# Loading one group's keys and queries as two halves, a value load moved ahead of a weight load, and six dummy matmuls fewer

## The chip, the cores and the metric

The kernel runs on one core of one Trainium2 chip. The metric is the device time of one execution, in microseconds (us). Before the change it is 399.24 us, the median of three runs (399.11 to 399.49). All runs quoted here count as fast (none is over 1.5% above the fastest of its kernel).

## The reference

Attention with eight heads over 4 batches of 768 rows feeds a mixture of four experts. Heads 0, 2 and 6 ("retrieval") are causal over everything. The other five ("stream") see four sink rows and a window of 64.

```python
# q, k, v: (4, 8, 768, 64)
scores = (q @ k.transpose(0, 1, 3, 2)) / 8
mask   = causal                            # heads 0, 2, 6
mask   = causal & (is_sink | in_window)    # the other heads
a      = softmax(where(mask, scores, -1e9))
x      = (a @ v).transpose(0, 2, 1, 3).reshape(3072, 512)
p      = domain_probs / domain_probs.sum(-1)
out    = sum(p[:, e] * (relu(x @ w1[e]) @ w2[e]) for e in range(4))
# w1[e]: (512, 1024), w2[e]: (1024, 512)
```

## The kernel before

The rows are worked on in eight groups of 384. For each group and each expert TensorE does 32 matmuls of the first layer (line L895) and 24 of the second (L919). The attention of group g+1 is interleaved into the experts of group g, so TensorE always has something to do, if the data is there. GpSimd issues the loads, in program order:

```python
    load_v(0, 0, [2, 1, 3, 4, 6])
    load_w1(0, 0, F)
    load_v(0, 0, [5, 7])
    load_w2(0)
    ...
    load_w1(1, 0, F)
    landed(w1_of(0))
    load_triples(k, k16, 0, 1)      # keys of group 1, all heads
    load_triples(q, qt16, 0, 1)     # queries of group 1, all heads
    landed(w2_of(0))
    load_w2(1)
    landed(qt16[0:1, 0, 0, 0:1])
    load_v(0, 1, RH)                # retrieval heads 0, 2, 6
    load_w1(2, 0, F)
    landed(w2_of(1))
    load_v(0, 1, SH[:2])            # stream heads 1, 3
    load_w2(2)
    load_v(0, 1, SH[2:])            # stream heads 4, 5, 7
    landed(w1_of(2))
    load_w1(3, 0, F)
    load_w2(3)
    # ... then, in the group loop, the keys, queries and values of group 2
```

`landed(x)` is a GpSimd copy of one element of a load's target, so GpSimd waits there for that load. One expert's `load_w1` is two loads (half the partitions each), `load_w2` is one. Below, w1(2) means the first-layer weights of expert 2.

For groups 0 and 1 TensorE transposes the keys and queries itself; from group 2 on the DMA does it, on SyncE's queue:

```python
        for j in range(3):
            nc.sync.dma_start(out=qTs[b, c][...], in_=q16[b, c][...], transpose=True)
        for x, xr in ((kR[i][:, c], kRr), (windows(kSf, c), kSr)):
            nc.sync.dma_start(out=x..., in_=xr..., transpose=True)
```

In the first attention TensorE runs dummy matmuls ahead of some heads' values, so that it isn't idle while it waits:

```python
            if first:
                warm_up(ps, {3: 4, 4: 4, 5: 6, 7: 10}.get(h, 0), 256)
```

The last tile of all is done in two column halves of 256, so that the first half's store starts sooner. A number `begin` for each group says after how much expert work the next group's attention is mixed in.

The softmax here doesn't subtract the row's maximum and nothing guards it: scores larger than these inputs give would overflow.

Of the kernel before, what the change touches and what calls it, by code (L numbers as in the profile page):

```python
# [17 lines left out]
def kernel(  # L18
# [33 lines left out]
    nc = tc.nc  # L52
    P = 128
    B, H, S, D = q.shape
    E, DM, F = moe_w1.shape
    CH = 3 * P
    NCH = S // CH
    N = B * S
    HP = H // 2
# [9 lines left out]
    RH = [h for h in range(H) if RETR[h]]  # L69
# [80 lines left out]
    def half(u):  # L150
        return slice(u * D, (u + 1) * D)
# [5 lines left out]
    def own_v(h):  # L157
        return half(PLACE[h][1])
# [10 lines left out]
    def v_tiles(b, c, h):  # L169

        if RETR[h]:
            return vR[b % 2][:, 3 * c : 3 * c + 3, RH.index(h), :]
        if b:
            return windows(vSf, c)[:, :, SH.index(h), :]
        return vS[:, c, :, SH.index(h), :]
# [10 lines left out]
    def rows_of(x, b, h, c):  # L186
        return x[b, h, c * CH : (c + 1) * CH, :].rearrange("(j p) d -> p j d", p=P)

    def tiles_of(x, b, h, c):
        return x[b, h, c * CH : (c + 1) * CH, :].rearrange("(t r) d -> r t d", r=TK)  # L190

    def windows_of(x, b, h, c):

        assert b > 0
        first = ((b * H + h) * S + c * CH - WO) * D
        return bass.AP(x.tensor, x.offset + first, [[D, P], [WQ * D, WT], [1, D]])
# [10 lines left out]
        q16[b, c] = att.tile([P, 3, H, D], FP16, name="q16", bufs=2)  # L207
        load_by_rows(q, q16[b, c], b, c)

    def load_triples(x, dst, b, c):  # L210

        gp.dma_start(
            out=dst.rearrange("p h j d -> p h (j d)"),
            in_=x[b, :, c * CH : (c + 1) * CH, :].rearrange(
                "h (p j) d -> p h (j d)", j=3
            ),
        )
# [47 lines left out]
    def load_v(b, c, heads):  # L265
        for h in heads:
            t = v_tiles(b, c, h)
            if RETR[h]:
                gp.dma_start(out=t[:, :, 0:D], in_=rows_of(v, b, h, c))  # L269
            elif b:  # L270
                gp.dma_start(  # L271
                    out=t[:, :, own_v(h)], in_=windows_of(v, b, h, c)
                )
            else:
                gp.dma_start(  # L275
                    out=t[R0:P, :, own_v(h)],
                    in_=tiles_of(v, b, h, c),
                )
# [18 lines left out]
    def load_w1(e, f0, f1):  # L297
        x = moe_w1[e].rearrange("(u c d) f -> u d c f", u=2, c=DMP)
        for u in range(2):
            gp.dma_start(  # L300
                out=w1sb[half(u), e * DMP : (e + 1) * DMP, f0:f1],
                in_=x[u, :, :, f0:f1],
            )
# [47 lines left out]
    for h in range(H):  # L351
        if h == 2:
            nc.sync.dma_start(
                out=v_s32, in_=v[0, :, 0:NS, :].rearrange("h r d -> r h d")
# [13 lines left out]
        eng = nc.scalar if h < HP else nc.sync  # L368
        eng.dma_start(out=q32[:, :, h, :], in_=rows_of(q, 0, h, 0))
    nc.sync.dma_start(  # L370
        out=probs, in_=moe_domain_probs.rearrange("(t p) e -> p t e", p=P)
# [14 lines left out]
    def warm_up(ps, n, cols):  # L386
        for _ in range(n):
            nc.tensor.matmul(
                out=ps[:, 0:cols], lhsT=warm[:, 0:P], rhs=warm[:, 0:cols],
                start=True, stop=True,  # L390
            )
# [53 lines left out]

    mask_c(bC, 0.0, -60000.0)
    mask_s(bS[:, 0:2, :], 2, 0.0, -60000.0)
    load_v(0, 0, [2, 1, 3, 4, 6])
    load_w1(0, 0, F)
    load_v(0, 0, [5, 7])  # L450
    load_w2(0)
    zero(gp, kR[0][:, 1, :, :, :])
    zero(gp, kS[:, 1, :, :, :].rearrange("p t s x -> p s t x"))
# [1 line left out]
    k16 = att.tile([P, H, 3, D], FP16, name="k16", bufs=1)  # L455
    qt16 = att.tile([P, H, 3, D], FP16, name="q16", bufs=2)

    def landed(x):

        gp.tensor_copy(out=seen, in_=x)  # L460
# [4 lines left out]
    def w2_of(e):  # L465
        return w2sb[0:1, e * FTP, 0:1]

    load_w1(1, 0, F)
    landed(w1_of(0))
    load_triples(k, k16, 0, 1)  # L470
    load_triples(q, qt16, 0, 1)
    landed(w2_of(0))
    load_w2(1)
    landed(qt16[0:1, 0, 0, 0:1])
    load_v(0, 1, RH)
    load_w1(2, 0, F)
    landed(w2_of(1))
    load_v(0, 1, SH[:2])
    load_w2(2)
# [15 lines left out]
    def attention(b, c):  # L495
        g = b * NCH + c
# [212 lines left out]
        def values(h):  # L709
            if RETR[h]:  # L710
                yield from values_r(h)
                return
            ct, u = PLACE[h]
            if first and u == 1:
                ps = pO.tile([P, 512], FP32, name="pO", bufs=2)
            else:
                ps = pV.tile([P, 512], FP32, name="pV", bufs=2)
            if first:
                warm_up(ps, {3: 4, 4: 4, 5: 6, 7: 10}.get(h, 0), 256)
            work = []  # L720
            for es, parts in es_of[h]:
                for t, o, q0, nq in parts:
                    work.append((es, t, o, q0, nq))
            ns = 0
            for n, (es, t, o, q0, nq) in enumerate(work):
                nc.tensor.matmul(  # L726
                    out=ps[:, q0 : q0 + nq],
                    lhsT=v_tile(b, c, h, t),
                    rhs=es[:, o : o + nq],
                    start=(n == 0),  # L730
                    stop=(n == len(work) - 1),
                    skip_group_check=True,
                )
                ns += mm_ns(nq)
                if ns > 300 and n < len(work) - 1:
                    yield ns
                    ns = 0

            r, o = half(u), half(1 - u)
            pair = first and h in (3, 4)  # L740
            if not pair or u == 0:
                rc_of[0] = att.tile([P, CH], FP32, name="rc", bufs=4)
            rc = rc_of[0]
            nc.scalar.activation(  # L744
                out=rc[r, :], in_=ps[o, 0:CH], func=AF.Ln, bias=eps[o, :]
            )

            def scale(r=r, ps=ps):
                nc.vector.tensor_tensor(  # L749
                    out=xT[g][r, ct, :], in0=ps[r, 0:CH], in1=rc[r, :], op=ALU.mult  # L750
                )

            if not pair:
                nc.scalar.activation(out=rc[r, :], in_=rc[r, :], func=AF.Exp, scale=-1.0)  # L754
                later(scale)
            elif u == 0:
                scale_of[0] = scale
            else:
                nc.scalar.activation(out=rc, in_=rc, func=AF.Exp, scale=-1.0)
                later(scale_of[0])  # L760
                later(scale)

            yield ns + (600.0 if g == 1 else 0.0)
# [92 lines left out]

    def last_tile(e, nt, hs, acc):

        for n, eng in enumerate((nc.sync, nc.scalar)):
            cols = slice(n * DM // 2, (n + 1) * DM // 2)  # L860
            ps = pV.tile([P, 512], FP32, name="pV", bufs=2)
            for ft in range(FTP):
                nc.tensor.matmul(
                    out=ps[:, 0 : DM // 2],
                    lhsT=hs[:, ft, 2 * P : 3 * P],
                    rhs=w2sb[:, e * FTP + ft, cols],
                    start=(ft == 0),
                    stop=(ft == FTP - 1),
                )
            nc.vector.scalar_tensor_tensor(  # L870
                out=acc[:, cols], in0=ps[:, 0 : DM // 2],
                scalar=p_sb[:, nt, e : e + 1], in1=acc[:, cols],
                op0=ALU.mult, op1=ALU.add,
            )
            eng.dma_start(out=out[nt * P : (nt + 1) * P, cols], in_=acc[:, cols])


    acc = {}
# [88 lines left out]
    UNIT = FTP * DMP * mm_ns(CH) + 3 * FTP * mm_ns(DM)  # L967
    for g in range(G):
        nxt = g + 1
        n_units = len(units[g])  # L970
        att_steps = iter(())
        if nxt < G:
            att_steps = attention(nxt // NCH, nxt % NCH)
        loads(g + 2)

        begin = {0: 1.15, 1: 1.0}.get(g, 0.0) * UNIT
        end = {0: 3.5}.get(g, 0.90 * n_units) * UNIT

        att_ns = 3500.0 if nxt % NCH == 0 else 5600.0
        if nxt < NCH:  # L980
            att_ns += 1100.0 + HP * 3 * 400.0 + NSH * 600.0
        spent = 0.0
        done = 0.0
        to_transpose = g + 2 < G
        for ns, share in moe_steps(units[g]):

            spent += ns * (share if g == 0 else 1.0)
            tick(ns)
            if to_transpose and spent > {0: 0.9, 1: 0.75}.get(g, 0.5) * n_units * UNIT:
                dma_transposes(*divmod(g + 2, NCH))  # L990
                to_transpose = False
            while done < (spent - begin) / (end - begin) * att_ns:
                step = next(att_steps, None)
                if step is None:
                    break
                done += step
                tick(step)
        for ns in att_steps:
            tick(ns)
        tick(LAG)  # L1000
# [35 lines left out]
```

## Time and profile before

| | before | where it is read |
|---|---|---|
| time, profiled run | 398.83 us | run |
| span | 397.1 us | cores |
| TensorE busy | 388.2 us | busy times |
| first L895 of group 0 | 22.09 us | TensorE timeline |
| w2(1), w1(2), w2(2), w2(3) landed | 39.8, 46.7, 53.2, 64.8 us | issue plus time to landing |
| start of the x32 block (32 matmuls in one row of the view) of L895 of group 1's first expert | 74.30 us | TensorE timeline |
| wait for group 2's transposed keys | 0.17 us, until 85.67 | TensorE timeline |

The main views are in the prediction. This is the timeline of GpSimd before (start, length, what was issued, and in brackets the idle time before it and what ended it):

```profile
41.71 0.91 POOL L306 DMA_DIRECT2D w2sb<-in_moe_w_dram  x1
...
65.13 1.02 POOL L227 DMA_DIRECT2D kSr<-in_k_dram  x1 [3.58 <-DMA w2sb<-in_moe_w_dram]
```

The load of w2(2) is issued at 41.71 with no wait. The last key load of group 2 is held 3.58 us by w2(3). No data pass between those two: the awaited load is the eighth before this one. The packed traces show why: GpSimd's loads, 144 before and 146 after, report their landing on eight semaphores (numbers 110 to 117), strictly in turn, and a load that has to wait is issued some 0.3 us after the load eight places ahead of it has landed (in the first 80 us of all fourteen profiles). Everything that GpSimd issues after this load moves with w2(3).

### The profile page before, as it was taken

How to read it: one execution, taken by the hardware profiler on the slowest of the kernel's cores; microseconds unless marked ns; L12 is line 12 of the kernel's file. 1: busy time of each engine (PE TensorE's matmuls, PEld its weight loads, DVE VectorE, ACT ScalarE, POOL GpSimd, SP SyncE). 2: the span in 40 equal slices, each digit the busy share in tenths (PEclk: the TensorE clock that was granted, in tenths of full speed). 3: DMA queues.
4: the chain of work that ended last, by engine and by line, in shares of the span. 5: the costliest groups of instructions: out<-in, count | busy, mean ns of one | idle time of the engine just before them, and what ended most of it. 6: DMA issues, size and time to landing. Idle time of an engine off the chain costs nothing.

```text
span 397.1 us, 7140 instructions
## 1 busy us (share of the span) xinstructions
PE 388.2 (98%) x2829; PEld 220.7 (56%) x2829; DVE 156.0 (39%) x344; ACT 219.0 (55%) x468; POOL 143.7 (36%) x184
## 2 busy tenths in 40 slices
PE   7899999999999999999999999999999999999996
PEld 4654556545555555555555555555555555555553
DVE  7734765324442234434332333433443223422222
ACT  4754569444766546655765446745564456853331
POOL 8833796808908706900049202940000000000000
PEclk9999999999999999999999999999999999999999
DMA  9999999999999999970779959990472000020002
GB/s 172 158 208 192 178 197 172 139 199 128 128 191 149 121 149 106 141 90 12 141 80 175 65 99 118 112 153 12 83 117 83 2 12 1 11 79 2 0 2 80
DMA packets 166133, 42.23 MB, mean 106 GB/s; under 512 B 156396, under 2 KB 161108, under 8 KB 166100
## 3 DMA queue, kind: packets, MB, share of 16 engines
q0 software_dynamic: 102656, 20.98, 62.0%
q1 hardware_dynamic: 61700, 20.27, 26.5%
q10 hardware_dynamic: 1744, 0.52, 0.6%
q8 instruction: 22, 0.36, 0.4%
q14 instruction: 11, 0.09, 0.1%
HBM read 43.57 MB, written 6.29 MB: 126 GB/s over the span
## 4 chain that ended last, share of the span: by engine, by line
PE 78%; DMA 15%; POOL 6%; issue 1%; DVE 0%; POOLq 0%
PE pA L895 35%; PE pO L919 35%; DMA w1sb<-in_moe_w_dram 4%; DMA w2sb<-in_moe_w_dram 4%; PE pA L614 4%; DMA q<-in_q_dram 3%; DMA kR<-kRr 2%; POOL vR L269 2%; PE pV L726 1%; PE pV L662 1%; DMA vS<-in_v_dram 1%; POOL w1sb L300 1%; POOL vS L275 1%; POOL vS L326 0%; POOL q L201 0%
## 5 line engine op out<-in xcount | busy, mean ns | idle before, releaser
L895 PE MATMUL pA<-xT,w1sb 128*128 128x384 f16 x1024 | 185.9, 326 | 0.1
L919 PE MATMUL pO<-w2sb,hs 128*128 128x512 f16 x760 | 179.0, 379 | 0.8 <-DMA w2sb<-in_moe_w_dram 0.8
L908 ACT ACTIVATE hs<-pA 128x384 f16<-128x384 f32 x256 | 121.8, 492 | 94.9 <-PE pA L895 89.6
L895 PEld LDWEIGHTS <-w1sb 128*128 128x128 f16 x1024 | 95.8, 98 | 59.6 <-issue 0.5
L919 PEld LDWEIGHTS <-hs 128*128 128x128 f16 x760 | 70.7, 98 | 73.9 <-DMA w2sb<-in_moe_w_dram 1.2
L632 ACT ACTIVATE es<-pA 128x384 f16<-128x384 f32 (+2 forms) x122 | 60.1, 512 | 53.7 <-PE pA L614 52.4
L935 DVE SCALAR_TENSOR_TENSOR acc<-pO,p_sb,acc 128x512 f32<-128x512 f32 x71 | 53.3, 751 | 71.8 <-PE pO L919 71.3
L227 POOL DMA_DIRECT2D kSr<-in_k_dram x30 | 30.1, 1006 | 31.5 <-DMA kS<-kSr 22.1
L223 POOL DMA_DIRECT2D kRr<-in_k_dram x18 | 14.1, 785 | 67.7 <-DMA kR<-kRr 67.7
L749 DVE TENSOR_TENSOR xT<-pV,rc 64x384 f16<-64x384 f32 x37 | 20.5, 554 | 32.0 <-ACT rc L754 24.3
L271 POOL DMA_DIRECT2D vS<-in_v_dram x30 | 30.4, 1024 | 0.8 <-DMA q<-in_q_dram 0.8
L931 DVE TENSOR_SCALAR acc<-pO,p_sb 128x512 f32<-128x512 f32 x24 | 18.0, 751 | 28.8 <-PE pO L919 28.6
L636 DVE TENSOR_TENSOR es<-es,mC 128x256 f16<-128x256 f16 (+1 forms) x42 | 10.9, 258 | 45.4 <-ACT es L632 44.3
L744 ACT ACTIVATE rc<-pV,eps 64x384 f32<-64x384 f32 x37 | 21.3, 575 | 12.1 <-PE pV L726 11.5
L614 PE MATMUL pA<-qT,kR 128*128 128x384 f16 (+2 forms) x120 | 24.4, 278 | 0.9 <-ACT qT L525 0.4
L754 ACT ACTIVATE rc<-rc 64x384 f32<-64x384 f32 x38 | 19.8, 521 | 1.2
L269 POOL DMA_DIRECT2D vR<-in_v_dram x24 | 19.2, 802 | 0.4 <-issue 0.3
L726 PEld LDWEIGHTS <-vS 128*128 128x128 f16 x255 | 13.4, 98 | 7.7 <-DMA vS<-in_v_dram 2.1
L636 DVE TENSOR_TENSOR es<-es,mW 128x384 f16<-128x384 f16 x30 | 10.7, 358 | 16.9 <-ACT es L632 16.8
L614 PEld LDWEIGHTS <-kR 128*128 128x128 f16 x120 | 11.4, 98 | 10.6 <-DMA kR<-kRr 0.6
L662 PEld LDWEIGHTS <-es 128*128 128x128 f16 x252 | 13.2, 97 | 6.9 <-ACT es L632 0.6
L614 PEld LDWEIGHTS <-kS 128*128 128x128 f16 x255 | 13.3, 98 | 6.6
(102 smaller groups left out, 188.4 us busy)
## 6 DMA issues: line engine op xcount, KB each, us to landing
out_dram<-acc SPq DMA_DIRECT2D x23, 256.0 KB
w1sb<-in_moe_w_dram POOLq DMA_DIRECT2D x8, 512.0 KB, 9.4
w2sb<-in_moe_w_dram POOLq DMA_DIRECT2D x4, 1024.0 KB, 13.2
kSr<-in_k_dram POOLq DMA_DIRECT2D x30, 112.0 KB, 3.8
vS<-in_v_dram POOLq DMA_DIRECT2D x30, 112.0 KB, 5.6
q<-in_q_dram POOLq DMA_DIRECT2D x18, 128.0 KB, 4.3
vR<-in_v_dram POOLq DMA_DIRECT2D x24, 48.0 KB, 4.4
kRr<-in_k_dram POOLq DMA_DIRECT2D x18, 48.0 KB, 3.7
```

Of the source, the lines that this page charges most:

```text
L227: gp.dma_start(out=kSr[:, :, SH.index(h), own(h)], in_=windows_of(k, b, h, c),)
L269: gp.dma_start(out=t[:, :, 0:D], in_=rows_of(v, b, h, c))
L271: gp.dma_start(out=t[:, :, own_v(h)], in_=windows_of(v, b, h, c))
L614: nc.tensor.matmul(out=ps[:, o : o + nq], lhsT=key_tile(b, c, h, t), rhs=qTs[b, c][:, hp, q0 : q0 + nq], start=(n == 0 or not first), stop ...
L632: nc.scalar.activation(out=es[:, 0:cols], in_=ps[:, 0:cols], func=AF.Exp, scale=SC)
L636: nc.vector.tensor_tensor(out=es[:, o0:o1], in0=es[:, o0:o1], in1=m[:, mo : mo + o1 - o0], op=ALU.mult,)
L744: nc.scalar.activation(out=rc[r, :], in_=ps[o, 0:CH], func=AF.Ln, bias=eps[o, :])
L749: nc.vector.tensor_tensor(out=xT[g][r, ct, :], in0=ps[r, 0:CH], in1=rc[r, :], op=ALU.mult)
L895: nc.tensor.matmul(out=pss[ft][:, 0:CH], lhsT=w1sb[:, e * DMP + ct, ft * P : (ft + 1) * P], rhs=xT[g][:, ct, :], start=(n == 0), stop=(n = ...
L908: nc.scalar.activation(out=hs[:, ft, :], in_=ps[:, 0:CH], func=AF.Relu)
L919: nc.tensor.matmul(out=ps_o, lhsT=hs[:, ft, j * P : (j + 1) * P], rhs=w2sb[:, e * FTP + ft, :], start=(ft == 0), stop=(ft == FTP - 1),)
L935: nc.vector.scalar_tensor_tensor(out=acc[nt], in0=ps_o, scalar=p_ap, in1=acc[nt], op0=ALU.mult, op1=ALU.add,)
```

## The change

The intent: let the first expert start sooner, let w2(1) land sooner, and pay for it with queries that are needed later.

```diff
-    def load_triples(x, dst, b, c):
+    def load_triples(x, dst, b, c, h0, h1):       # heads h0 to h1 only
 ...
-    load_v(0, 0, [2, 1, 3, 4, 6])
+    load_v(0, 0, [2, 1, 3, 4, 6, 5])
     load_w1(0, 0, F)
-    load_v(0, 0, [5, 7])
+    load_v(0, 0, [7])
 ...
-    load_triples(k, k16, 0, 1)
-    load_triples(q, qt16, 0, 1)
+    load_triples(k, k16, 0, 1, 0, HP)             # heads 0 to 3
+    load_triples(q, qt16, 0, 1, 0, HP)
     landed(w2_of(0))
     load_w2(1)
     landed(qt16[0:1, 0, 0, 0:1])
-    load_v(0, 1, RH)
     load_w1(2, 0, F)
+    load_v(0, 1, RH[:2])
+    load_triples(k, k16, 0, 1, HP, H)             # heads 4 to 7
+    load_triples(q, qt16, 0, 1, HP, H)
+    load_v(0, 1, RH[2:])
 ...
-                warm_up(ps, {3: 4, 4: 4, 5: 6, 7: 10}.get(h, 0), 256)
+                warm_up(ps, {3: 4, 4: 4, 5: 6, 7: 4}.get(h, 0), 256)
 ...
-        for n, eng in enumerate((nc.sync, nc.scalar)):
-            cols = slice(n * DM // 2, (n + 1) * DM // 2)
+        for c0, c1, eng in ((0, 3 * P, nc.sync), (3 * P, DM, nc.scalar)):
+            cols = slice(c0, c1)
 ...
-        begin = {0: 1.15, 1: 1.0}.get(g, 0.0) * UNIT
+        begin = {0: 1.05, 1: 1.0}.get(g, 0.0) * UNIT
```

The last tile's columns, 384 + 128 instead of 256 + 256, and the smaller `begin` come with it.

More of the change, by code (lines that the diff above doesn't have):

```diff
@@ L208, in load_q @@
         load_by_rows(q, q16[b, c], b, c)
-    def load_triples(x, dst, b, c):
+    def load_triples(x, dst, b, c, h0, h1):
         gp.dma_start(
-            out=dst.rearrange("p h j d -> p h (j d)"),
-            in_=x[b, :, c * CH : (c + 1) * CH, :].rearrange(
+            out=dst[:, h0:h1, :, :].rearrange("p h j d -> p h (j d)"),
+            in_=x[b, h0:h1, c * CH : (c + 1) * CH, :].rearrange(
                 "h (p j) d -> p h (j d)", j=3
@@ L863, in last_tile @@
                 nc.tensor.matmul(
-                    out=ps[:, 0 : DM // 2],
+                    out=ps[:, 0 : c1 - c0],
                     lhsT=hs[:, ft, 2 * P : 3 * P],
@@ L870, in last_tile @@
             nc.vector.scalar_tensor_tensor(
-                out=acc[:, cols], in0=ps[:, 0 : DM // 2],
+                out=acc[:, cols], in0=ps[:, 0 : c1 - c0],
                 scalar=p_sb[:, nt, e : e + 1], in1=acc[:, cols],
```

## The prediction

> **What bounds the kernel now.** I read the page first, then the waits, then the TensorE timeline where the waits sit, then the landing time of each load.
>
> ```profile
> PE 388.2 (98%) x2829; PEld 220.7 (56%) x2829; DVE 156.0 (39%) x344; ACT 219.0 (55%) x468; POOL 143.7 (36%) x184
> ...
> PE 78%; DMA 15%; POOL 6%; issue 1%; DVE 0%; POOLq 0%
> ```
>
> TensorE is busy for 98% of the span, and the chain that ended last stays on it from 85.67 us onward; only before that do loads carry the chain. So a gain must come from the first 86 us: from idle TensorE, or from dummy matmuls, which count as busy. From 100 to 380 us TensorE is busy all the time, so what is won or lost early is kept to the end. The waits of TensorE:
>
> ```profile
> PE pO L726 <- DMA vS<-in_v_dram: 1.2, 1, 1.2
> PE pO L919 <- DMA w2sb<-in_moe_w_dram: 0.8, 1, 0.8
> ...
> PE pA L614 <- DMA kR<-kRr: 0.2, 1, 0.2
> ```
>
> They are three places. In the TensorE timeline (start, length, what, idle before):
>
> ```profile
> 18.33 0.82 PE L388 MATMUL pO<-warm 128*128 128x256 f16 x6
> 20.32 0.42 PE L726 MATMUL pO<-es,vS 128*128 128x160 f16 x4 [1.18 <-DMA vS<-in_v_dram]
> 20.58 0.33 PE L703 MATMUL pV<-ident,x_pair 128*128 128x128 f16 x3
> 20.75 1.25 PE L388 MATMUL pO<-warm 128*128 128x256 f16 x10
> 21.84 0.41 PE L726 MATMUL pO<-es,vS 128*128 128x160 f16 x4
> 22.09 5.75 PE L895 MATMUL pA<-xT,w1sb 128*128 128x384 f16 x32
> ...
> 39.82 1.04 PE L919 MATMUL pO<-w2sb,hs 128*128 128x512 f16 x4 [0.81 <-DMA w2sb<-in_moe_w_dram]
> ...
> 46.44 0.36 PE L516 MATMUL pA<-ident,q 128*64 128x128 f16 x6
> ...
> 85.67 0.39 PE L614 MATMUL pA<-qT,kR 128*128 128x128 f16 x2 [0.17 <-DMA kR<-kRr]
> ```
>
> Head 5's values hold TensorE until 20.32; ten dummies (1.09 us) then stand before head 7's values, so the first expert starts at 22.09. The second expert's second layer waits for w2(1) until 39.82. The line at 46.44 has no wait: it transposes heads 6 and 7 of group 1's queries.
>
> GpSimd issues the loads. Issue time plus time to landing gives these landings: head 5's values 20.3, head 7's 20.6, w1(0) 20.1, w2(0) 25.5, w1(1) 30.5, group 1's keys 32.6, its queries 34.8, w2(1) 39.8, three retrieval values 40.1 to 40.8, w1(2) 46.6, w2(2) 53.2, w2(3) 64.8. They land in the order of issue, each as soon as the ones before it are through. This is one full queue: a weight megabyte takes about 5.0 us (39.8 minus 34.8), keys or queries 2.15 us. The three values and w1(2) take 6.85 us together, so with 5.1 for w1(2) a value load costs 0.58.
>
> **What the Trainium skill says.** "DMA: Bandwidth & Descriptors", section "Anatomy of one DMA — SWDGE (gpsimd) path": DMA engines do not wait on semaphores; they just consume their queues. The landings agree: order of issue decides, and a load moved forward gains exactly what it overtakes. The same page, "Specifications", wants at least 512 B per transfer for line rate. The values are written in rows of 64 fp16, 128 B; while they passed (38 to 40 us) the rate was 137 GB/s, against 206 in the two microseconds before. "TensorE: Matmul & The Clock Gate", section "Part 1: The HAM clock gate": half clock after at least one idle window of about 3.4 us. The trace has no idle as long after its start and the granted clock stays 1.00, so it cannot confirm the threshold, but 1.18 us idle did no harm. The same page, "Wait — 56ns, not 53.3ns?": N/2.4 GHz plus 2.5 ns, 216 ns at 512 columns; four L919 matmuls start 0.86 us apart here, so I use 0.216 us, and 0.163 for 384 columns.
>
> **The change, part by part.**
>
> *Start.* Head 5's values now are issued at about 10.3 instead of 11.5 and no longer stand behind w1(0), so they land near 16. The matmuls before end with six dummies at 18.33 + 6 x 0.109 = 18.98, and head 5 follows at once. The transposes of the pair need VectorE's x_pair, ready at 19.62; four dummies (0.44) end near 20.4. Head 7's values still land at 20.6, since the bytes before them are the same; their matmuls end near 20.9. w1(0) lands some 0.3 later, about 20.4. The first expert thus starts at about 20.95 instead of 22.09: 1.15 us gained. It is not the sum 1.18 + 0.65, because head 7 becomes the wait.
>
> *w2(1).* Half of keys and queries, 2.15 us of the queue, no longer stand before it: 25.55 + 4.95 + 2.15 + 5.0 = 37.65. The first halves land at 31.6 and 32.65. TensorE begins the second expert at 32.86 - 1.15 - about 0.05 = 31.65. The program order of the changed kernel puts the first query transposes after 8 L895 matmuls (20 before), at 31.65 + 1.3 = 32.95: just after their landing. Then 24 L895 (3.9) and three groups of transposes (0.29 each) bring it to 37.75, when w2(1) is there. The wait of 0.81 goes, so up to here some 1.9 us are gained.
>
> *The second halves.* In the changed order 16 L919 matmuls (3.45), 14 score matmuls (1.6) and one group of key transposes follow, and the transposes of heads 6 and 7 come up near 43.3. They read the second halves, which now stand behind w1(2) and two value loads. In the queue: w2(1) 37.65, w1(2) 5.1, two values 1.16, second keys 1.07, second queries 1.07: they land at about 46.0. TensorE stands for some 2.7 us. Before, the same transposes began at 46.44 with 20 L919 done; the change has 16 done, so the place of equal progress is 46.44 - 4 x 0.216 = 45.58. The changed kernel is then 46.0 - 45.58 = 0.4 us *behind*. The early gains turn into waiting.
>
> *From there to 86 us* the work is the same in another order, and TensorE had no wait there. w1(2) lands earlier (42.8); w2(2) and later loads have the same bytes ahead, so w2(3) stays near 64.8. The key transposes for group 2 (85.6) start behind an output store that waits for TensorE's result, so they shift with it. The 0.4 stays.
>
> *Last tile.* 384 + 128 columns instead of 256 + 256 give equal matmul columns. VectorE took 0.48 us for 256 columns and 0.75 for 512: 0.62 and 0.34 by interpolation. The first can start near 393.05, both end near 394.0, as before (393.99). The stores leave closer together instead of 0.7 us apart: 0 to 0.3 us later; I take 0.1.
>
> Sum: 399.24 + 0.4 + 0.1 = 399.7.
>
> **Rivals.** (1) *No stall at the second halves.* If they land before 43.5, the 1.9 us are kept until the key transposes for group 2, which TensorE already waited for by 0.17. These can move too, as the store ahead of them on the queue waits on VectorE's accumulation, but their queries land at 70.7 to 72.4 whatever TensorE does: I would expect 1.0 to 1.6 of the 1.9 to survive, 397.8 to 398.3. For it speaks that the author chose this place; against it the queue sum above. Chance 15%. (2) *A partial stall,* the halves at 45.0 to 45.5: 0.1 to 0.6 ahead, 398.8 to 399.2. A packing of the queue better by 5% does this; chance 25%. (3) *The stall cools the clock.* If 2.7 us of idle are enough, about 3.4 us at half clock cost 1.7 more: 401.4. The window of the page speaks against it; chance 7%. (4) *w2(3) and all behind it land earlier,* because the issue waits are shorter: hidden, the queue was never empty.
>
> **Range and chances.** The centre is drawn slightly toward rivals 1 and 2: 399.5. Most of the error is the landing of the second queries, 0.7 us either way, and the tail, 0.2. Range 398.1 to 400.7. Two per cent is 8 us, more than all waits of TensorE together; even the cooled clock stays within it. Faster 0.01, within 0.98, slower 0.01.
>
> **What would show it.** Right: first L895 near 21.0; no wait for w2(1); a new TensorE wait of 2 to 3 us on the load of the queries at its transposes near 43 to 46; w1(2) landed some 3 us before use; the wait for group 2's transposed keys about as before. Wrong: no wait at those transposes, or the second queries landing well before 45; a first L895 after 21.5 (head 7 or w1(0) later); granted clock under 1.00 after the stall; or a wait at the group 2 keys that grows by as much as the start gained, which would say that the loads and not TensorE set the time there.

## More of the kernel before

From the chain of waits before, the part that leads to group 2's keys (start, length):

```profile
48.48 16.36 DMA w2sb<-in_moe_w_dram
...
77.97 7.65 DMA kR<-kRr
```

w2(3) is on its way from 48.48 to 64.84, and the transposes of group 2's retrieval keys take 7.65 us and end at 85.62, when TensorE is already waiting.

## The result, and the profile after

Before and after ran in four rounds: before 399.18 us (median of 399.02 to 399.49), after **400.08 us** (400.57, 399.68, 400.23, 399.92). A ratio is the mean time of one kernel's fast runs over the mean of the runs of before, so it is not quite the ratio of the medians: here 1.0022, with a 95% interval of 1.0005 to 1.0039. By the 2% criterion it is the same; within that it is a little slower. The profiled run is the slowest of the four, 400.57, with a span of 398.8 against 397.1.

The kernel was run again later, in six rounds (e12): 399.84 (399.24 to 400.77), ratio 1.0016 (1.0000 to 1.0033).

The page of after, busy times and chain:

```profile
PE 388.0 (97%) x2823; PEld 220.0 (55%) x2823; DVE 156.3 (39%) x344; ACT 219.4 (55%) x468; POOL 144.3 (36%) x186
...
PE 77%; DMA 15%; POOL 6%; issue 1%; DVE 0%; DVEq 0%; POOLq 0%
```

TensorE has six matmuls fewer and is busy 0.2 us less, in a span that is 1.7 us longer. So the difference is idle time of TensorE. Its waits after (in total, how often, the longest):

```profile
PE pA L519 <- DMA q<-in_q_dram: 1.7, 1, 1.7
PE pA L617 <- DMA kR<-kRr: 1.6, 1, 1.6
...
PE pO L922 <- DMA w2sb<-in_moe_w_dram: 0.2, 1, 0.2
```

The wait of 1.2 for head 5's values is gone, and of the 0.8 for w2(1) 0.2 is left. In their place stand 1.7 for the second queries and 1.6 for group 2's keys. The TensorE timeline after, at the same places as in the prediction (lines of the kernel are shifted by three, so L895 is now L898):

```profile
18.91 0.41 PE L729 MATMUL pO<-es,vS 128*128 128x160 f16 x4
...
19.77 0.60 PE L388 MATMUL pO<-warm 128*128 128x256 f16 x4
20.41 0.42 PE L729 MATMUL pO<-es,vS 128*128 128x160 f16 x4
20.67 5.79 PE L898 MATMUL pA<-xT,w1sb 128*128 128x384 f16 x32
...
38.22 1.02 PE L922 MATMUL pO<-w2sb,hs 128*128 128x512 f16 x4 [0.20 <-DMA w2sb<-in_moe_w_dram]
...
45.53 0.36 PE L519 MATMUL pA<-ident,q 128*64 128x128 f16 x6 [1.66 <-DMA q<-in_q_dram]
...
87.26 0.39 PE L617 MATMUL pA<-qT,kR 128*128 128x128 f16 x2 [1.59 <-DMA kR<-kRr]
```

The first expert starts 1.42 us earlier (20.67 against 22.09). Second-layer work of the second expert starts 1.60 earlier (38.22 against 39.82). At 45.53 all of that is spent on waiting for the second queries: the place of equal progress before is 45.58, by the prediction's working. In both kernels the x32 block (32 matmuls in one row of the view) of L895 of group 1's first expert then begins at nearly the same time, 74.30 before and 74.48 after. At group 2's keys TensorE stands 1.59 instead of 0.17. The sum: 0.18 up to the x32 block, 1.42 at the keys, 0.1 in the last tile (from its expert's last sixteen full-width matmuls to the end of the span 9.09 us, against 8.99) is 1.70, and the spans differ by 1.7.

The timeline of GpSimd after tells why the loads behind are later:

```profile
40.43 0.67 POOL L275 DMA_DIRECT2D vS<-in_v_dram  x1 [0.93 <-DMA w1sb<-in_moe_w_dram]
42.94 0.90 POOL L306 DMA_DIRECT2D w2sb<-in_moe_w_dram  x1 [1.84 <-DMA w1sb<-in_moe_w_dram]
...
66.34 1.02 POOL L227 DMA_DIRECT2D kSr<-in_k_dram  x1 [4.23 <-DMA w2sb<-in_moe_w_dram]
```

With two loads more in the sequence, the load eight places before w2(2) is the second part of w1(2), a large one just issued. Before it was w2(1), which GpSimd had already waited for. So w2(2) is issued at 42.94 instead of 41.71, and w2(3) lands at 66.0 instead of 64.8. How the one leads to the other is not shown. From 44 to 46 and from 46 to 48 us after moves 148 and 155 GB/s, less than e4 below, where w2(2) is issued early (195 and 209); but before moves no more in the second stretch (170 and 155), and in the first 1105 packets of after are 128-byte pieces of value loads (610 in before), which bring few bytes each. The chain of waits after:

```profile
47.21 18.84 DMA w2sb<-in_moe_w_dram
...
78.08 9.13 DMA kR<-kRr
```

w2(3) is issued earlier than before (47.21 against 48.48) and still lands later. The transposes of the keys are issued at about the same time as before (78.08 against 77.97), but take 9.13 instead of 7.65 us.

### The profile page after: what moved, and what is told of

Its sections match the earlier page's. It is cut to its first block, busy times and chain, and to the rows that moved or that the text cites. A ratio compares the mean times of both kernels' runs of the same rounds, so it can differ in the third digit from the quotient of the medians.

```text
span 398.8 us, 7128 instructions
## 1 busy us (share of the span) xinstructions
PE 388.0 (97%) x2823; PEld 220.0 (55%) x2823; DVE 156.3 (39%) x344; ACT 219.4 (55%) x468; POOL 144.3 (36%) x186
## 4 chain that ended last, share of the span: by engine, by line
PE 77%; DMA 15%; POOL 6%; issue 1%; DVE 0%; DVEq 0%; POOLq 0%
PE pA L898 35%; PE pO L922 35%; DMA w2sb<-in_moe_w_dram 5%; DMA w1sb<-in_moe_w_dram 4%; PE pA L617 4%; DMA q<-in_q_dram 3%; DMA kR<-kRr 2%; PE pV L729 1%; PE pV L665 1%; POOL vS L275 1%; POOL vR L269 1%; DMA vS<-in_v_dram 1%; POOL q L201 1%; POOL w1sb L300 1%; POOL vS L326 0%
## 5 line engine op out<-in xcount | busy, mean ns | idle before, releaser
L898 PE MATMUL pA<-xT,w1sb 128*128 128x384 f16 x1024 | 185.9, 326 | 0.1
L898 PEld LDWEIGHTS <-w1sb 128*128 128x128 f16 x1024 | 95.9, 98 | 60.0 <-issue 0.6
```

Source lines behind the costliest of these rows:

```text
L898: nc.tensor.matmul(out=pss[ft][:, 0:CH], lhsT=w1sb[:, e * DMP + ct, ft * P : (ft + 1) * P], rhs=xT[g][:, ct, :], start=(n == 0), stop=(n = ...
```

## The experiments

Twelve runs were made, of nine new kernels (e1 to e9) and three repeats, each correct. The second call (e5 to e8) was on another chip than the other two. Three reasons were to be told apart. First, that the wait for the second queries takes the gain of the start. Second, that the loads behind set the time, because w2(2) is held and w2(3) and group 2's loads come later. Third, that a stall of some 2 us lowers the granted clock. (Letters in the expectations: A is the wait for the second queries; B and C are rivals that put the loss on the loads behind it.) The medians of before are 399.44 and 399.71.

| run | what | median, us | range | ratio to before (95%) |
|---|---|---|---|---|
| e1 | before + new start | 400.61 | 398.60–400.72 | 1.0015 (0.9996–1.0035) |
| e2 | halves only | 399.69 | 398.73–399.87 | 1.0004 (0.9992–1.0017) |
| e3 | second halves ahead of w1(2) | 397.25 | 397.01–397.82 | 0.9951 (0.9938–0.9963) |
| e4 | w2(2) issued sooner | 399.19 | 398.58–400.67 | 1.0000 (0.9984–1.0015) |
| e5 | two value loads ahead of w1(2) | 400.74 | 398.75–401.26 | 1.0019 (0.9995–1.0043) |
| e6 | group 2's attention later | 400.14 | 399.29–400.44 | 1.0012 (0.9994–1.0030) |
| e7 | e3 with the old last tile | 396.66 | 396.58–397.16 | 0.9932 (0.9915–0.9949) |
| e8 | e3 with the old start | 398.27 | 397.85–398.72 | 0.9970 (0.9950–0.9989) |
| e9 | e5 with dummies in the wait | 399.25 | 398.92–399.82 | 1.0002 (0.9989–1.0014) |
| e10 | e3 again | 397.08 | 396.92–397.94 | 0.9951 (0.9937–0.9964) |
| e11 | e7 again | 397.37 | 396.88–397.86 | 0.9952 (0.9937–0.9966) |
| e12 | after again | 399.84 | 399.24–400.77 | 1.0016 (1.0000–1.0033) |

### e1: the new start alone

```diff
 # from before
-    load_v(0, 0, [2, 1, 3, 4, 6])
+    load_v(0, 0, [2, 1, 3, 4, 6, 5])
     load_w1(0, 0, F)
-    load_v(0, 0, [5, 7])
+    load_v(0, 0, [7])
-    warm_up(ps, {3: 4, 4: 4, 5: 6, 7: 10}...)
+    warm_up(ps, {3: 4, 4: 4, 5: 6, 7: 4}...)
```

> The kernel before with head 5's values ahead of w1(0) and six dummies fewer, nothing else. My theory (the loads set the time at the group 2 keys, so what TensorE wins before 86 us is lost): the first expert starts near 20.7 us, the wait for w2(1) grows from 0.8 to about 2.0 us because w2(1) still lands near 39.8, and the time is that of the kernel before within 0.2 us. Rival (a gain early is kept to the end): 397.9 to 398.2.

Measured: 398.60 and 398.64 in two runs, 400.59 to 400.72 in the other four; the profile fell on one of the long ones. Its TensorE timeline:

```profile
40.38 1.04 PE L919 MATMUL pO<-w2sb,hs 128*128 128x512 f16 x4 [2.28 <-DMA w2sb<-in_moe_w_dram]
...
41.81 3.50 PE L919 MATMUL pO<-w2sb,hs 128*128 128x512 f16 x8
```

In this run the gain of the start goes into the wait for w2(1), which grows from 0.81 to 2.28 us. That was expected. The second line was not: the same eight matmuls took 1.90 us in before. The windows of e1 (stretch, its length, then busy time and count of TensorE, weight loads, VectorE, ScalarE and GpSimd, then granted clock, DMA share and GB/s):

```profile
42.00:44.00 2.00, 2.00 (x6) 0.76 (x5) 1.97 (x3) 0.00 (x0) 2.00 (x4) 0.50 1.11 188
44.00:46.00 2.00, 2.00 (x11) 1.01 (x9) 0.77 (x2) 0.35 (x1) 1.21 (x2) 0.66 1.24 187
```

The clock is at half for about 3.4 us: 2.0 in the first stretch and, at a mean of 0.66, some 1.36 in the second. The mean clock over the span is 0.996 in three of the four long runs, 0.999 and 1.000 in the two short ones. One long run (400.59) shows 1.000, and I can't explain that one. The two short runs are 0.8 us below the median of before (399.44; one run of before, 398.50, is as short), so it stays open whether the new start alone is worth nothing where the clock holds.

### e2: the halves alone

```diff
 # from after: the start, the dummies and the last tile as in before
```

> The kernel before with the halves and the earlier begin of the attention steps, without the start and the last tile. My theory: the first expert starts at 22.1, no wait for w2(1), a wait for the second queries of 0.5 to 1 us, the wait for the group 2 keys at 1 us or more, since w2(3) lands near 66 as in the changed kernel; the time is near the changed kernel's, 399.7 to 400.2. Rival (the halves are what the change gains, and another part costs): under 399.

Measured: 399.69, the same as before within 0.2%. No wait for w2(1) is left, and TensorE stands for 1.10 us where it needs the second queries, which land at 45.66. So what the halves gain at w2(1) and lose at the second queries cancels without the start, too. The wait for group 2's keys is 0.66 us here, where 1 or more was expected.

### e3: the second halves ahead of w1(2)

```diff
 # from after
+    load_triples(k, k16, 0, 1, HP, H)
+    load_triples(q, qt16, 0, 1, HP, H)
     load_w1(2, 0, F)
     load_v(0, 1, RH[:2])
-    load_triples(k, k16, 0, 1, HP, H)
-    load_triples(q, qt16, 0, 1, HP, H)
```

> The changed kernel with the second halves of keys and queries ahead of w1(2). No wait of TensorE at their transposes (they land near 40). Theory A (the wait at the second queries costs the time): 398.2 to 398.6. Theory B (the transposed keys of group 2 set the time, TensorE only arrives there earlier): the wait there grows to 3 us or more and the time is at least 399.2, the kernel before's, less only what an earlier w2(3) brings.

Measured: 397.25, 0.5% faster than before, with all five runs below the fastest run of before. TensorE waits for no load after 21 us. From its timeline:

```profile
72.96 5.36 PE L898 MATMUL pA<-xT,w1sb 128*128 128x384 f16 x32
...
83.99 0.38 PE L617 MATMUL pA<-qT,kR 128*128 128x128 f16 x2
```

The x32 block begins 1.34 us earlier than in before (74.30), and at group 2's keys (83.99) there is no wait. The second queries land at 40.0 instead of 45.5, w1(2) at 45.0 instead of 42.6, and it is first used near 47: it had that slack. w2(2) is issued at 40.29 and w2(3) lands at 63.3, so both the wait for the queries and the delay of the loads behind are gone at once. The gain is larger than the 398.2 to 398.6 that the first reason alone gave.

### e4: w2(2) issued sooner

```diff
 # from after
     landed(w2_of(1))
-    load_v(0, 1, SH[:2])
     load_w2(2)
+    load_v(0, 1, SH[:2])
```

> The changed kernel with w2(2) issued before the values of heads 1 and 3, so that it waits for w2(1) and not for the second part of w1(2): issued near 39 instead of 42.9. Theory C (that late issue let the queue run thin and moved w2(3) from 64.8 to 66.0): w2(3) lands near 64.8 to 65.2 again, the wait for the group 2 keys falls from 1.6 to under 0.7 us, time near 399.2. Rival (the issue wait is hidden, the order or the run made the loads slower): w2(3) stays at 65.7 or later and the time at 399.8 to 400.2.

Measured: 399.19, ratio 1.0000. w2(2) is issued at 38.69 and w2(3) lands at 63.5 instead of 66.0. The wait for the second queries stays, the one for group 2's keys goes:

```profile
45.86 0.36 PE L519 MATMUL pA<-ident,q 128*64 128x128 f16 x6 [1.97 <-DMA q<-in_q_dram]
...
85.83 0.38 PE L617 MATMUL pA<-qT,kR 128*128 128x128 f16 x2
```

So the later issue of w2(2) is what delays w2(3) (e5 tests this in a second way), and the two waits are separate: one can be taken away without the other. One of the six runs, the longest (400.67), has a clock of 0.995.

### e5: two value loads ahead of w1(2)

```diff
 # from after
+    load_v(0, 1, RH[:2])
     load_w1(2, 0, F)
-    load_v(0, 1, RH[:2])
```

> The changed kernel with the two value loads put before w1(2) instead of behind it. The order in which the loads lie in the queue stays else the same, and the second queries still land near 45.5 us; but the load of w2(2) now shares its semaphore with a value load that lands near 39 and not with w1(2)'s second part, so it is issued near 40.5 instead of 42.9. Theory C (the late issue of w2(2) is what slowed the loads after it): w2(3) lands near 64 to 65 instead of 66.0, no or little wait for the group 2 keys, 399.0 to 399.4. Rival D (the order of small loads before w2(2) slowed them, which only the exchange in the run before had changed): w2(3) at 65.7 or later, wait for the keys above 1 us, 399.8 to 400.2.

This leaves every load of after and nearly its order, but another load now stands eight places before w2(2). GpSimd's timeline in e5:

```profile
40.40 0.91 POOL L306 DMA_DIRECT2D w2sb<-in_moe_w_dram  x1
41.88 0.69 POOL L275 DMA_DIRECT2D vS<-in_v_dram  x1 [0.57 <-DMA w1sb<-in_moe_w_dram]
44.35 0.67 POOL L275 DMA_DIRECT2D vS<-in_v_dram  x1 [1.78 <-DMA w1sb<-in_moe_w_dram]
45.39 0.67 POOL L275 DMA_DIRECT2D vS<-in_v_dram  x1 [0.37 <-DMA k<-in_k_dram]
```

w2(2) no longer waits. The two value loads behind it wait for the two parts of w1(2), and the next one for the second keys: each time exactly the eighth load before. w2(3) lands at 64.2, and the wait for group 2's keys is gone. That much came as expected. Over all fourteen profiles, w2(3) lands at 63.3 to 65.0 where w2(2) is issued by 42.3 us, and at 66.0 to 66.5 where it is issued at 42.9 or later. The time did not: 400.46 to 401.26 in four runs at a clock of 0.994 to 0.996, and 398.75 and 399.08 in two at 0.999. The TensorE timeline of a long one:

```profile
46.29 0.36 PE L519 MATMUL pA<-ident,q 128*64 128x128 f16 x6 [2.20 <-DMA q<-in_q_dram]
...
48.14 1.89 PE L922 MATMUL pO<-w2sb,hs 128*128 128x512 f16 x4
```

Four second-layer matmuls take 1.89 us; the same four take 1.04 in e9, at full clock.

### e6: group 2's attention mixed in later

```diff
 # from after
-        begin = {0: 1.05, 1: 1.0}.get(g, 0.0) * UNIT
+        begin = {0: 1.05, 1: 1.4}.get(g, 0.0) * UNIT
```

> The changed kernel with the first attention step of group 2 put off from 1.0 to 1.4 units, about 4 us more of expert matmuls ahead of the wait for its keys. If the wait for the keys is what makes the changed kernel slower than the kernel before: no wait there, 398.8 to 399.3, that is the kernel before's time, and not less, since the wait at the second queries still takes the early gain. Rival (the wait at the second queries alone makes it slower): still near 400.

Measured: 400.14, and 399.89 in the profiled run; 398.8 to 399.3 was expected, so this is a miss. The wait for group 2's keys did go. In its place there is one for ScalarE at the second layer:

```profile
116.40 4.22 PE L922 MATMUL pO<-w2sb,hs 128*128 128x512 f16 x18 [0.48 <-ACT hs L911]
```

The profiled run is 0.68 us below that of after, which is less than half of the 1.59; the median doesn't show a gain at all. Putting the use later gives part of the wait back elsewhere.

### e7, e8: e3 with the old last tile, and with the old start

```diff
 # e7, from e3: the last tile 256 + 256 as in before
 # e8, from e3: load_v(0, 0, [2, 1, 3, 4, 6]) ... [5, 7], ten dummies, as in before
```

> The fast variant (second halves ahead of w1(2)) with the last tile in 256 + 256 columns as before. The trace has the last tile 0.1 us longer in 384 + 128, so 397.15 against 397.25; rival (384 + 128 helps): 397.4 or more.

> The fast variant without the start (head 5's values behind w1(0) again, ten dummies). TensorE begins the first expert 1.2 us later and nothing waits for a load after that: 398.3 to 398.5. Rival (a later load hides the start again, so that the start is worth nothing): 397.3.

Measured: e7 396.66, e8 398.27. The start makes the difference between e3 and e8. In e8's timeline the old wait for head 5 is back:

```profile
20.70 0.42 PE L729 MATMUL pO<-es,vS 128*128 128x160 f16 x4 [1.72 <-DMA vS<-in_v_dram]
...
22.47 5.75 PE L898 MATMUL pA<-xT,w1sb 128*128 128x384 f16 x32
```

The first expert starts 1.2 us later than in e7 (21.26), and so does the x32 block (74.15 against 72.94). The time is 1.6 longer than e7's (which has the old tail), and 0.9 to 1.2 longer than that of e3, e10 and e11. They were run on another chip. So the start is worth some 0.9 to 1.6 us once no later load takes it back. In e1 four runs of six showed nothing of it.

### e9: dummies in e5's wait

```diff
 # from e5, in the transposes by TensorE
+                if not first and hp == 3 and not is_k:
+                    warm_up(ps, 12, 384)
```

> The variant with two value loads ahead of w1(2), and twelve dummy matmuls of 384 columns (1.95 us) in TensorE's wait for the second queries, so that it is not idle there but waits just as long. Theory E (where the granted clock fell to half after that wait, the run lost about 1.7 us; without the fall the better loads show): all runs near 398.7 to 399.1, clock at least 0.998 in each. Rival (the slower runs of that variant came from the loads): still 400 or more in most runs.

The twelve dummies stand where TensorE waited for the second queries:

```profile
43.86 2.11 PE L388 MATMUL pA<-warm 128*128 128x384 f16 x12
```

Nothing useful is done sooner: the transposes start at 45.99 (e5: 46.29). Measured: 398.92 to 399.82 in six runs, four of them above the 399.1 expected, the clock at 0.999 or above in all. The median falls by 1.5 us from e5's, on another chip; against before the ratio goes from 1.0019 to 1.0002. This speaks for the idle time, and not the wait itself, as what cost e5 its long runs; e5 was not run beside e9, so it is not shown beyond doubt.

### e10, e11, e12: the two tails again, and after again

```diff
 # e10: e3 unchanged.  e11: e7 unchanged.  e12: after unchanged.
```

> The fast variant again, beside the next run on the same chip, to measure the last tile: with 384 + 128 columns 0.1 to 0.6 us slower than with 256 + 256.

> The fast variant with the last tile of before, beside the run above. 396.6 to 397.1, and 0.993 to 0.994 of the kernel before: faster than both kernels.

> The changed kernel itself once more, with five rounds on the chip of the others. Ratio to the kernel before 1.0005 to 1.004 as in the first result. In its runs the granted clock stays at 1.00 as in the first four, or, if a wait of 1.7 us can also bring it down, some runs are at 0.995 and 1.5 us or more slower.

Measured: 397.08 with 384 + 128 columns, 397.37 with 256 + 256, and the means are 397.33 and 397.37. Between e3 and e7 the sign was the other way. Both expectations were missed: the last tile has no effect that these runs can show. The version of e3 beats before and after, by 0.5% against before; e7 is it with the old tail.

e12 fell on a quick run of after, 399.24, and its TensorE timeline is worth a look:

```profile
46.02 0.36 PE L519 MATMUL pA<-ident,q 128*64 128x128 f16 x6 [1.55 <-DMA q<-in_q_dram]
...
86.00 0.38 PE L617 MATMUL pA<-qT,kR 128*128 128x128 f16 x2
```

The wait for the second queries is there again, while that for group 2's keys isn't. Yet w2(2) was again held (issued at 43.92) and w2(3) landed late, at 66.5; and the transposes were issued at 78.58, half a microsecond later than in the first profile. They took at most 7.42 us instead of 9.13 (7.28 by the semaphore records of the packed trace). So a late w2(3) does not by itself bring the wait at the keys. The profiled runs differ by 1.33 us in time and by 1.3 in span, and the wait of 1.59 is in the longer one alone.

## Why the prediction was right, and where it was not

The time, 400.08 and in the repeat 399.84, lies in the range of 398.1 to 400.7, and "same" was given 0.98. The centre of 399.5 was too low by 0.6 and 0.3.

**Start.** Right. Predicted was a first expert at 20.95; it came at 20.67. Head 5's values landed at 14.2 (near 16 predicted), and neither head 7 nor w1(0) (20.1) held TensorE as long as feared. The gain was 1.42 for 1.15. e7 against e8 shows that it is real, and e1's profile that on its own it can be lost to w2(1).

**w2(1).** Right, at 38.2 for 37.65, with a wait of 0.20 where none was forecast. In e12 it landed at 38.8 and the wait was 0.75: this part of the gain varies between runs.

**The second halves.** Right in mechanism, off in size. The prediction had the second queries landing at 46.0 after a wait of 2.7. They landed at 45.5, and TensorE came to them later, so it waited 1.66. The term of 0.4 us behind was in fact 0.05 ahead. In part that is luck: w2(1) landed 0.5 us later than predicted, while w1(2), the two values and the halves took 7.30 us for the predicted 8.40 (w1(2) 4.48 for 5.1, a value load 0.33 for 0.58; the prediction's own landings, 40.1 to 40.8 for three values after 39.8, gave about 0.34). e3 shows what it costs to have them behind w1(2): with them ahead of it, the kernel is 2.8 us faster than after (e10 against e12), though that also brings the loads behind forward.

**From there to 86 us.** This is the step that failed. It said that "w2(2) and later loads have the same bytes ahead, so w2(3) stays near 64.8". It landed at 66.0. The bytes were the same, but the number of loads was not, and with it changed which load w2(2) has to wait for before it may be issued. e4 and e5 take that wait away in two ways, one by order and one by which load stands eight places before. Both bring w2(3) back to 63.5 and 64.2. Rival 4 had the same flaw from the other side: "hidden, the queue was never empty". The moment of issue does matter, and the rule that a load moved forward "gains exactly what it overtakes" had left it out.

The next sentence, that the key transposes "shift with it" and so the 0.4 stays, held only for their issue: the store ahead of them moved from 71.83 to 72.00 with TensorE, and they moved by 0.11. But their length grew by 1.48 and TensorE waited 1.42 longer. The prediction had taken their length as fixed. By the semaphore records of the packed traces it is anything from 4.15 us (e5) to 9.17 (e6, which has the loads of after). The range still held the result, but it was drawn for the landing of the second queries and the tail, not for this.

I had first taken the late w2(3) to be the cause, since it pushes group 2's value loads into the time of these transposes. e12 has the same late loads without the wait: it comes with after in one profile of two, not at all in e4 and e5, at 0.66 in e2 and at 0.32 in e10, whose w2(3) is early. The packed traces show a second candidate. In before, after and e12 some 20 packets of the transposes, which mostly take about 18 ns each, take 1.3 to 1.5 us all at once, in a block that begins some 0.4 us after a 16 KB packet of the instruction queue (1.0 to 1.1 us). In after the block lasts from 85.74 to 87.24: 13 of the 16 parts of the key transposes had landed by 85.58, and the last three came at 87.19 to 87.21. In before it lies within them, too (84.02 to 85.38), and in e12 it begins at 86.03, just after they had landed (85.86). Without the block those of after would have ended near 85.6 and those of before near 84.3 (an estimate: 85.62 less 1.36), so the late loads may well lengthen them, and e12 does not speak against it. No run separates the two, and none with these transposes alone was made: what decides the length stays open.

**Last tile.** 0.1 was predicted and 0.10 is what the two traces give; the times can't resolve it.

**The clock** (rival 3, given 7%). In the profiled after the clock stays at 1.00 through both waits of 1.6 us, so it does not explain the result. But the argument against this rival was wrong. With 2.2 us idle the clock did drop, in e1 and e5, for about the 3.4 us that the rival assumed, and e9 speaks for the idle time as its cause. One run of six of e12 has 0.996 (400.69) and one of six of e4 0.995 (400.67), so waits of 1.5 to 2.0 us may now and then do it, too. A few runs of before show 0.994 to 0.996 as well, for a reason I don't know.

## What to carry to other kernels

A gain before a wait for a load is kept only if that load moves, too: the new start went into the wait for w2(1) in e1's profile and was worth some 0.9 to 1.6 us once the second halves stood ahead of w1(2), a megabyte which had slack. Adding a load instruction, even with no byte more, changes which older load each later one waits for, so read GpSimd's waits again and not only the bytes in the queue. Where TensorE must wait for some 2 us in its full-speed stretch, dummy matmuls in the wait look like cheap insurance (e9 against e5).

## What the Trainium skill lacked or had wrong

- "TensorE: Matmul & The Clock Gate", section "Part 1: The HAM clock gate", gives half clock after at least one idle window of about 3.4 us. Here 2.28 us (e1) and 2.20 us (e5) of idle before matmuls were enough: clock 0.50 in the window of 42 to 44 us of e1, and a mean clock of 0.994 to 0.996 in three of six runs of e1 and four of six of e5. Filled with dummies (e9), none of six has it.
- "DMA: Bandwidth & Descriptors" says that a semaphore wait happens on the issuing sequencer, before dispatch, but not that GpSimd's loads share eight completion semaphores in turn, so that the issue of one can be held by the load eight places earlier in the program. Here that moved w2(2)'s issue from 40.40 (e5) to 42.94 us, and w2(3)'s landing from 64.2 to 66.0.
- No page that I read says how far the time of a DMA transpose of fp16 tiles varies beside other loads: the same transposes, from issue to landing, took 7.65 us in before, 9.13 in the first profile of after, 7.28 in the second and 4.15 in e5. Nor does one that I read tell of some 20 transpose packets held for 1.3 to 1.5 us beside a packet of the instruction queue.
